# Half of the input weights by a second queue, decays turned earlier, and low parts by a product: a fused RWKV and convolutional expert kernel

## The chip, the cores and the metric

The kernel runs on one core of one Trainium2 chip. The metric is the device time of an execution in microseconds; the runs of a kernel are told by their median.

## The reference

Inputs are r, k, v, w of shape (4, 8, 768, 48) (batch, heads, steps, head size), u of (8, 48) and three weight arrays in float64: w_in (384 x 1024), conv_w (3 x 1024) and w_out (1024 x 384). For every batch and head a 48 x 48 state runs over the 768 steps:

```
y[t]  = r[t] @ (state + outer(u * k[t], v[t]))
state = w[t][:, None] * state + outer(k[t], v[t])
```

The 8 heads of a step are put side by side as a row x of 384. Then

```
h    = relu(x @ w_in)
conv = sum over j of conv_w[j] * h[t - 1 + j]      (zeros outside the sequence)
out  = (h * sigmoid(conv)) @ w_out
```

## The kernel before

The steps are cut into 24 chunks of 128 (6 for each batch). A chunk has two stages. Stage A (`stage_a`, line 531) loads w, k, r, v of the chunk with 128 partitions of 8 x 48 values (`loads`, L514, issued by SP). For each of w, k, r an ACT copy (L540) rearranges the last two heads, and three PE transposes (L546) turn the tile. DVE scans the turned decays from the end (L553), takes a reciprocal of three columns (L557, into a dA buffer), scales the keys (L558), scans from the start (L560) and scales r (L564). In the first four chunks (EARLY) the last pair of heads is gathered by twelve matmuls (L573) and an ACT copy into `last` (L576), later by six small transfers (L581). POOL forms z = r * k * u (L588, L590), DVE sums it (L591) and POOL writes it as the diagonal of pm (L594). Keys are turned back (L602, copies L604 and L605). Two ACT passes check w's bounds (L610).

Stage B (`stage_b`, line 614) carries the state. Scores go to two banks (L667; those of the last pair read `last`), DVE copies the part above the diagonal into pm (L671), the new state is made (L684, L688), and y is summed in one bank. In the first four chunks ACT copies y rounded to the reduced float32 format as the high part of x (L715), and DVE subtracts that from y to get the low part (L716). In later chunks this goes by L738 and L740.

The product stage (`block`, line 792) runs for every 384 steps, 8 blocks in all. Each of the 8 slices of 128 hidden columns takes nine matmuls (L760: three row blocks, each as high x high, high x low, low x high), the gating on ACT, DVE and POOL (L772 to L782), and the second product (L789) with an ACT copy and a store (L819, L820).

Weights arrive as float64 and are converted once, in the middle of the first chunks. w_in goes in three blocks m (`win_pieces`, line 477). Block m lands in one buffer by four transfers that SP issues: 48 rows into partitions 0 to 47 (L484), 16 rows into 48 to 63 (L488), 48 rows into 64 to 111, 16 rows into 112 to 127; a row is 8 KB. A block is then converted in three pieces of 384, 384 and 256 columns: DVE takes exponent and mantissa (L442, L450), ACT scales the exponent (L445), DVE joins them (L447, L453), POOL multiplies (L456), ACT rounds (L462), POOL takes the low part (L463). conv_w takes the same way (L470 to L475), w_out comes in three transfers of 128 partitions (L499) and eight pieces.

u is loaded ahead of everything by ACT's queue (L340); after five warm-up matmuls on zeros (L347) a product with a row of ones spreads it over the partitions (L363), and ACT copies it (L586).

The order of the instructions on each engine is written by a planner (class `Plan`, line 112). Each operation has a length from a table, tokens that it reads and writes, buffers that it holds, and a rank. The planner steps through a modelled time; a free engine takes the ready operation of the lowest rank whose buffers are to be had. Ranks are 14 for each chunk (stage B 7 later, loads 10 earlier), 10 + 5 j for piece j of w_in, 60 + 5 j for w_out, and the block's own for products. Transfers go through a model of the queues (class `Wire`, line 79). The order is then fixed: on the chip each engine runs its instructions in it and waits where data is late.

Of the kernel before, what the change touches and what calls it, by code (L numbers as in the profile page):

```python
# [9 lines left out]
F32 = mybir.dt.float32  # L10
# [12 lines left out]
WARM = 5  # L23

CHUNK, LEAD, UNIT, DOWN, PIECE = 14.0, 0.0, 5.0, 1.6, 5.0
FIRST_IN, FIRST_OUT = 10.0, 60.0
AHEAD, GUARD = 10.0, 10.0
SPREAD = (3, 5)
EARLY = 4
COLD = 60.0  # L30
CAPS = (4, 5, 3, 3, 4)
GT, TB = 1, 1
WIN = 2.0
# [8 lines left out]
    gather=1.6, carried_rows=1.4, y_rows=1.5,  # L42
    load=0.55, issue=0.45, spread=0.64,
)
TAIL = dict(PE=0.22, DVE=0.11, ACT=0.13, POOL=0.07, SP=2.2)
# [33 lines left out]
class Wire:  # L79
# [8 lines left out]
    def add(self, q, work, i, at):  # L88

        over = sum(x[0] for x in self.queues[q]) - 4.6  # L90
        self.queues[q].append([work, i, at])
        return max(0.0, over)

    def next(self):

        heads = self.heads()
        times = [q[0][2] for q in self.queues.values() if q and q[0][2] > self.t + 1e-9]
        times += [self.t + h[0] * len(heads) for h in heads]
        return min(times, default=float("inf"))
# [12 lines left out]
class Plan:  # L112
# [29 lines left out]
    def issue(self):  # L142
# [8 lines left out]
        free = dict.fromkeys(engines, 0.0)  # L151
# [5 lines left out]
        events, order, t = [], [], 0.0  # L157
# [17 lines left out]
        while len(order) < n:  # L175
            for e in engines:
# [10 lines left out]
                if e == "PE" and t < COLD:  # L187
                    us *= 1.4
# [13 lines left out]
            for i in wire.advance(t):  # L202
                heapq.heappush(events, (t + TAIL["SP"], i))
# [96 lines left out]
def rwkv_conv_moe_kernel(  # L300
# [38 lines left out]
    wide = ([fconst.tile([P, HB], F32, name=f"wide{i}") for i in range(4)], [])  # L339
    nc.scalar.dma_start(out=wide[0][0][0:1, :], in_=u.rearrange("h d -> (h d)").unsqueeze(0))  # L340


# [13 lines left out]
    make_identity(nc, ident)  # L356
    ones_f = fconst.tile([P, P], F32, name="ones_f")
# [5 lines left out]
    nc.tensor.matmul(banks[-1][:, 0:H * D], lhsT=ones_f[0:1, :], rhs=wide[0][0][0:1, :], start=True, stop=True)  # L363
# [24 lines left out]

    def kind(name, n, shape, dtype=F32, fill=None):
# [11 lines left out]
    dA_k = kind("dA", 2, [P, WID], fill=lambda t: nc.vector.memset(t, 0.0))  # L401
# [64 lines left out]
    def load_conv():  # L466
# [4 lines left out]
            out=raw.t.bitcast(I32)[0:rows, 0:2 * P], in_=conv_w.rearrange("j (t c) -> (j t) c", t=FT)), [], [(raw, 0)], [raw], moves=0.2)  # L471
# [5 lines left out]
    def win_pieces(m, piece):  # L477
# [19 lines left out]
    def wout_pieces(t0, n, piece):  # L497
# [3 lines left out]
            [], [(raw, 0)], [raw], moves=0.95 * n)  # L501
# [7 lines left out]
    def loads(n):  # L509
# [21 lines left out]
    def stage_a(n):  # L531
# [7 lines left out]
        def tr(src, t, cols):  # L539
# [4 lines left out]
            def f():  # L544
                for m in range(KT):
# [4 lines left out]
        wp, kp, rp = Buf(pa), Buf(pa), Buf(pa)  # L550
        op("DVE", "pad", lambda: nc.vector.memset(wp.t[:, 0:WID:SL], 0.0), [], [(wp, 1)], [wp])
# [3 lines left out]
            op0=ALU.mult, op1=ALU.add), [wp, (wp, 1)], [kr])  # L555
        tr(K_, kp, lambda m: kp.t[:, m * L:(m + 1) * L])
# [8 lines left out]
                                                        op=ALU.mult), [rp], [(kr, 1)], [kr])  # L565
        if n < EARLY:
# [11 lines left out]
        else:  # L578
            for g in range(2):
                for m in range(KT):  # L580
# [3 lines left out]
                        [last], moves=0.05)  # L584
# [29 lines left out]
    def stage_b(n):  # L614
# [78 lines left out]
        if early:  # L693
# [22 lines left out]
            op("DVE", "kt", lambda: nc.vector.tensor_tensor(  # L716
# [132 lines left out]
    for n in range(N + 1):  # L849
        if n < N:  # L850
# [66 lines left out]
```

## Time and profile before

| what | value |
|---|---|
| median of 3 runs | 382.01 us (379.9 to 383.73) |
| profiled execution | 381.53 us |
| its span, first to last instruction | 379.8 us |
| PE busy | 354.3 us (93%) |
| DVE busy | 281.5 us (74%) |
| ACT busy | 235.0 us (62%) |
| POOL busy | 174.9 us (46%) |
| mean granted clock of PE | 0.971 |

The span is shorter than the execution's time by 1.7 us, which lie before the first and after the last instruction. Busy shares are means over stages that differ, so the stages are to be read apart.

### The profile page before, as it was taken

How to read it: one execution, taken by the hardware profiler on the slowest of the kernel's cores; microseconds unless marked ns; L12 is line 12 of the kernel's file. 1: busy time of each engine (PE TensorE's matmuls, PEld its weight loads, DVE VectorE, ACT ScalarE, POOL GpSimd, SP SyncE). 2: the span in 40 equal slices, each digit the busy share in tenths (PEclk: the TensorE clock that was granted, in tenths of full speed). 3: DMA queues.
4: the chain of work that ended last, by engine and by line, in shares of the span. 5: the costliest groups of instructions: out<-in, count | busy, mean ns of one | idle time of the engine just before them, and what ended most of it. 6: DMA issues, size and time to landing. Idle time of an engine off the chain costs nothing.

```text
span 379.8 us, 7861 instructions
## 1 busy us (share of the span) xinstructions
PE 354.3 (93%) x2790; PEld 323.0 (85%) x2790; DVE 281.5 (74%) x575; ACT 235.0 (62%) x613; POOL 174.9 (46%) x199
## 2 busy tenths in 40 slices
PE   7977679878899999999999999999999999999994
PEld 4856568767698998999999999998999998999993
DVE  5697799998997887488787865798679845864640
ACT  6264574877768473588766753688566525765741
POOL 7293587675964343165643440454553410233430
PEclk9978888998999999999999999999999999999999
DMA  8999993322325444542542443934054121010001
GB/s 161 182 186 177 230 275 72 65 53 63 72 59 111 85 96 82 107 97 54 102 103 51 80 100 70 191 64 97 29 104 94 31 52 56 0 44 21 22 22 66
DMA packets 112802, 34.44 MB, mean 91 GB/s; under 512 B 103069, under 2 KB 110774, under 8 KB 112374
## 3 DMA queue, kind: packets, MB, share of 16 engines
q1 hardware_dynamic: 112756, 33.89, 42.0%
q8 instruction: 23, 0.38, 0.4%
q14 instruction: 21, 0.17, 0.2%
q10 hardware_dynamic: 2, 0.00, 0.0%
HBM read 25.19 MB, written 4.72 MB: 79 GB/s over the span
## 4 chain that ended last, share of the span: by engine, by line
PE 74%; DVE 9%; DMA 6%; issue 4%; ACT 3%; POOL 2%; SPq 1%; DVEq 0%; POOLq 0%
PE bank L789 26%; PE bank L760 24%; PE bank L733 5%; PE bank L667 5%; PE bank L546 4%; PE bank L723 4%; DMA r<-in_r_dram 4%; PE bank L684 2%; DMA k<-in_k_dram 2%; PE bank L602 2%; DMA wide<-in_moe_conv_w_dram 1%; DVE wide L447 1%; DVE g L779 1%; DVE a L774 1%; POOL wide L456 1%
## 5 line engine op out<-in xcount | busy, mean ns | idle before, releaser
L789 PE MATMUL bank<-wo,gh 128*128 128x384 f32 x576 | 125.7, 345 | 2.0 <-POOL wo L463 1.0
L760 PE MATMUL bank<-xT,wi 128*128 128x386 f32 x576 | 125.2, 346 | 0.2 <-DVE xT L716 0.2
L782 POOL TENSOR_TENSOR gh<-g,gh 128x384 fp32r<-128x384 f32 x64 | 64.5, 1012 | 107.2 <-ACT gh L781 104.2
L789 PEld LDWEIGHTS bank<-wo,gh 128*128 128x128 f32 x576 | 100.1, 189 | 4.9 <-issue 1.3
L760 PEld LDWEIGHTS bank<-xT,wi 128*128 128x128 f32 x576 | 100.2, 188 | 3.2 <-issue 1.8
L774 DVE SCALAR_TENSOR_TENSOR a<-bank,cw,a 128x384 f32<-128x384 f32 x64 | 38.3, 608 | 20.4 <-ACT a L773 20.4
L778 ACT ACTIVATE a<-a 128x384 f32<-128x384 f32 x64 | 33.3, 522 | 27.0 <-DVE a L776 27.0
L594 POOL TENSOR_SCALAR_AFFINE_SELECT pm<-dg 128x1024 f32<-128x1024 f32 x24 | 26.3, 1095 | 48.2 <-PE bank L733 38.7
L779 DVE TENSOR_TENSOR g<-bank,a 128x384 f32<-128x384 f32 x64 | 34.5, 547 | 13.8 <-ACT a L778 13.1
L772 ACT ACTIVATE bank<-bank 128x386 f32<-128x386 f32 x64 | 30.5, 477 | 22.1 <-PE bank L760 21.2
L781 ACT CAST gh<-g 128x384 fp32r<-128x384 f32 x64 | 32.4, 511 | 12.9 <-DVE g L779 12.6
L671 DVE COPY_PREDICATED pm<-upper,bank 128x512 f32<-128x512 int32 x48 | 33.4, 725 | 8.5 <-PE bank L667 8.4
L776 DVE SCALAR_TENSOR_TENSOR a<-bank,cw,a 128x384 f32<-128x384 f32 x64 | 38.5, 610 | 0.6
L773 ACT ACTIVATE a<-bank,cw 128x384 f32<-128x384 f32 x64 | 36.5, 580 | 0.6
L553 DVE TENSOR_TENSOR_SCAN kr<-bank,one_end 128x387 f32<-128x387 f32 x24 | 22.9, 956 | 15.0 <-PE bank L546 15.0
L588 POOL TENSOR_TENSOR z<-r,k 128x384 f32<-128x384 f32 x24 | 24.3, 1014 | 19.6 <-DMA r<-in_r_dram 19.6
L590 POOL TENSOR_TENSOR z<-z,ubc 128x384 f32<-128x384 f32 x24 | 24.2, 1007 | 1.3
L667 PEld LDWEIGHTS bank<-kr 48*128 48x128 f32 x288 | 18.7, 189 | 6.9 <-issue 4.5
L667 PE MATMUL bank<-kr 48*128 48x128 f32 x288 | 23.7, 291 | 0.5 <-DVE wide L453 0.4
L560 DVE TENSOR_TENSOR_SCAN kr<-bank,dA 128x387 f32<-128x387 f32 x24 | 22.8, 952 | 0.1
L733 PE MATMUL bank<-pm,v 128*48 128x128 f32 x320 | 22.3, 282 | 0.0
L819 ACT COPY wide<-bank 128x384 f32<-128x384 f32 x24 | 11.5, 479 | 16.4 <-PE bank L789 16.0
(108 smaller groups left out, 529.0 us busy)
## 6 DMA issues: line engine op xcount, KB each, us to landing
w<-in_w_dram SPq DMA_DIRECT2D x24, 192.0 KB, 2.9
k<-in_k_dram SPq DMA_DIRECT2D x24, 192.0 KB, 3.6
r<-in_r_dram SPq DMA_DIRECT2D x24, 192.0 KB, 3.8
v<-in_v_dram SPq DMA_DIRECT2D x24, 192.0 KB, 3.0
out_dram<-wide SPq DMA_DIRECT2D x24, 192.0 KB, 2.0
gh<-in_moe_w_in_dram SPq DMA_DIRECT2D x6, 384.0 KB, 6.5
gh<-in_moe_w_out_dram SPq DMA_DIRECT2D x2, 1152.0 KB, 7.4
last<-kr SPq DMA_DIRECT2D x120, 16.2 KB, 1.8
```

The costliest lines, as they stand in the source:

```text
L667: nc.tensor.matmul(sc[g].t[:, m * L:(m + 1) * L], lhsT=kt(m)[p], rhs=rt(m)[p], start=True, stop=True)
L671: op("DVE", "cp", lambda g=g: nc.vector.copy_predicated(out=pm.t[:, g], mask=upper.unsqueeze(1).to_broadcast([P, NP, L]), data=sc[g].t.rea ...
L733: nc.tensor.matmul(y.t[rows, cs], lhsT=vf[:, h * D:h * D + rows.stop - rows.start], rhs=pm.t[:, g, m, :], start=(c == 0 and m == 0), stop= ...
L760: nc.tensor.matmul(t.t[:, 0:HB + 2], lhsT=wi[:, m, a, f * P:(f + 1) * P], rhs=xT[:, x0 + m, c, xs], start=(m == 0 and j == 0), stop=(m == ...
L773: ("ACT", "mul", lambda: nc.scalar.mul(out=a(), in_=h(1), mul=cw[:, 1, bass.ds(f, 1)]), [t, "cw"], [a1]),
L774: ("DVE", "stt", lambda: nc.vector.scalar_tensor_tensor(out=a(), in0=h(0), scalar=cw[:, 0, bass.ds(f, 1)], in1=a(), op0=ALU.mult, op1=ALU. ...
L776: ("DVE", "stt", lambda: nc.vector.scalar_tensor_tensor(out=a(), in0=h(2), scalar=cw[:, 2, bass.ds(f, 1)], in1=a(), op0=ALU.mult, op1=ALU. ...
L778: ("ACT", "sig", lambda: nc.scalar.activation(out=a(), in_=a(), func=AF.Sigmoid), [], [a1]),
L779: ("DVE", "gate", lambda: nc.vector.tensor_tensor(out=g.t[:, 0:width], in0=h(1), in1=a(), op=ALU.mult), [t, a1], [g]),
L781: ("ACT", "cast", lambda: nc.scalar.copy(out=part(0)[:, 0:width], in_=g.t[:, 0:width]), [g], [key]),
L782: ("POOL", "lo", lambda: nc.gpsimd.tensor_tensor(out=part(1)[:, 0:width], in0=g.t[:, 0:width], in1=part(0)[:, 0:width].bitcast(F32), op=AL ...
L789: nc.tensor.matmul(acc.t[:, 0:DM], lhsT=part(a)[:, tt * P:(tt + 1) * P], rhs=wo[:, f, c, :], start=(f == 0 and a + c == 0), stop=(f == FT ...
```

## The change

The lower 48 rows of each w_in block stay on SP's queue, the upper 48 (partitions 64 to 111) are issued by ACT, block 0's after the copy of chunk 0's k, block m's after that of chunk m + 1's w. w_in's blocks and the filter weights are entered into the plan one chunk later, with ranks 14 + 6 j for w_in and 65 + 6 j for w_out. In chunks 1 to 3 padding, turning and first scan of the decays have a rank lower by 10. u is loaded by ACT as an operation of the plan, and its product stands behind chunk 0's turned r. There are nine warm-up matmuls, and one dA buffer. The low part of x in the first four chunks is made by a product of the high part with a negated identity, added into y's bank, and an ACT copy. The planner's model has other numbers: transfers have a share of the engines and places in a ring, and engines begin later. The diff, cut to its core:

```diff
-WARM = 5
+WARM = 9
-CHUNK, LEAD, UNIT, DOWN, PIECE = 14.0, 0.0, 5.0, 1.6, 5.0
-FIRST_IN, FIRST_OUT = 10.0, 60.0
+CHUNK, LEAD, UNIT, DOWN, PIECE = 14.0, 0.0, 5.0, 1.6, 6.0
+FIRST_IN, FIRST_OUT = 14.0, 65.0
-COLD = 60.0
+COLD = ((9.9, 1.8), (60.0, 1.3))
-WIN = 2.0
+RING = 192
+FIRST = 10.0
-TAIL = dict(PE=0.22, DVE=0.11, ACT=0.13, POOL=0.07, SP=2.2)
+TAIL = dict(PE=0.22, DVE=0.11, ACT=0.13, POOL=0.07, SP=1.4)
+BEGIN = dict(PE=4.3, DVE=2.4, ACT=3.0, POOL=5.0, SP=0.8)
...
-    def add(self, q, work, i, at):
-        over = sum(x[0] for x in self.queues[q]) - 4.6
-        self.queues[q].append([work, i, at])
-        return max(0.0, over)
+    def add(self, q, moves, i, at):
+        work, share, places = moves
+        over, held = sum(x[4] for x in self.queues[q]) + places - RING, 0.0
+        for x in self.queues[q]:
+            if over <= 0:
+                break
+            over -= x[4]
+            held += x[0]
+        self.queues[q].append([work, i, at + 0.7, share, places])
+        return held
+    def pace(self, heads):
+        return 1.0 / max(1.0, sum(h[3] for h in heads))
...
-                if e == "PE" and t < COLD:
-                    us *= 1.4
+                if e == "PE":
+                    us *= next((x for until, x in COLD if t < until), 1.0)
...
-                heapq.heappush(events, (t + TAIL["SP"], i))
+                heapq.heappush(events, (t + (0.8 if self.ops[i][5][2] == 64 else TAIL["SP"]), i))
...
-    nc.scalar.dma_start(out=wide[0][0][0:1, :], in_=u.rearrange("h d -> (h d)").unsqueeze(0))
...
+    less = fconst.tile([P, P], F32R, name="less")
+    nc.scalar.mul(out=less, in_=ident, mul=-1.0)
...
-    nc.tensor.matmul(banks[-1][:, 0:H * D], lhsT=ones_f[0:1, :], rhs=wide[0][0][0:1, :], start=True, stop=True)
...
-    dA_k = kind("dA", 2, [P, WID], fill=lambda t: nc.vector.memset(t, 0.0))
+    dA_k = kind("dA", 1, [P, WID], fill=lambda t: nc.vector.memset(t, 0.0))
...
-        for g in range(2):
-            op("SP", "issue", lambda g=g: nc.sync.dma_start(
+        for g, (eng, queue) in enumerate((("SP", nc.sync), ("ACT", nc.scalar))):
+            r0 = (6 + g) * D + 16 * m
+            op(eng, "issue", lambda g=g, queue=queue: queue.dma_start(
                 out=row()[64 * g:64 * g + D, 0:2 * DF], in_=w_in[(2 * m + g) * D:(2 * m + g + 1) * D, :]),
-                [], [(raw, 2 * g)], [raw], moves=WIN * 0.75)
-            r0 = (6 + g) * D + 16 * m
+                [(chunks[m + 1]["w"] if m else chunks[0]["k"], 1)] if g else [], [(raw, 2 * g)], [raw], moves=(2.3, 0.5, 4))
             op("SP", "issue", lambda g=g, r0=r0: nc.sync.dma_start(
                 out=row()[64 * g + D:64 * g + 64, 0:2 * DF], in_=w_in[r0:r0 + 16, :]),
-                [], [(raw, 2 * g + 1)], [raw], moves=WIN * 0.25)
+                [], [(raw, 2 * g + 1)], [raw], moves=(1.2, 0.5, 2))
...
         wp, kp, rp = Buf(pa), Buf(pa), Buf(pa)
+        rank = plan.rank
+        plan.rank = rank - (FIRST if 0 < n < EARLY else 0.0)
         op("DVE", "pad", lambda: nc.vector.memset(wp.t[:, 0:WID:SL], 0.0), [], [(wp, 1)], [wp])
         tr(W, wp, lambda m: wp.t[:, m * SL + 1:m * SL + 1 + L])
         op("DVE", "scan", lambda: nc.vector.tensor_tensor_scan(
...
             op0=ALU.mult, op1=ALU.add), [wp, (wp, 1)], [kr])
+        plan.rank = rank
         tr(K_, kp, lambda m: kp.t[:, m * L:(m + 1) * L])
...
+        if n == 0:
+            ut, row = Buf(pb), chunks["u"]
+            op("PE", "ones", lambda: nc.tensor.matmul(ut.t[:, 0:H * D], lhsT=ones_f[0:1, :], rhs=row.t[0:1, :],
+                                                      start=True, stop=True), [(R_, 1), row], [ut])
+            op("ACT", "kh", lambda: nc.scalar.copy(out=ubc.rearrange("p h d -> p (h d)"), in_=ut.t[:, 0:H * D]), [ut], ["ubc"])
...
-        if n == 0:
-            op("ACT", "kh", lambda: nc.scalar.copy(out=ubc.rearrange("p h d -> p (h d)"), in_=banks[-1][:, 0:H * D]),
-               [(K_, 1)], ["ubc"])
...
             op("ACT", "kh", lambda: nc.scalar.copy(out=xT[:, 0:KT, 0, ts], in_=thirds(y.t)), [y], [("x", odd, c, 0)])
-            op("DVE", "kt", lambda: nc.vector.tensor_tensor(
-                out=xT[:, 0:KT, 1, ts], in0=thirds(y.t), in1=xT[:, 0:KT, 0, ts].bitcast(F32), op=ALU.subtract),
-                [y, ("x", odd, c, 0)], [("x", odd, c, 1)])
+            op("PE", "rest", lambda: nc.tensor.matmul(thirds(y.t), lhsT=less, rhs=xT[:, 0:KT, 0, ts], start=False, stop=True,
+                                                      skip_group_check=True), [("x", odd, c, 0)], [y])
+            op("ACT", "kh", lambda: nc.scalar.copy(out=xT[:, 0:KT, 1, ts], in_=thirds(y.t)), [y], [("x", odd, c, 1)])
...
+    plan.rank = -2 * AHEAD
+    chunks["u"] = Buf(val_k)
+    op("ACT", "issue", lambda: nc.scalar.dma_start(out=chunks["u"].t[0:1, :], in_=u.rearrange("h d -> (h d)").unsqueeze(0)),
+       [], [chunks["u"]], moves=(0.05, 1.0, 4))
...
-            if n < KT:
-                plan.rank = FIRST_IN + PIECE * KT * n
-                win_pieces(n, piece)
-                if n == 0:
+            if 0 < n <= KT:
+                plan.rank = FIRST_IN + PIECE * KT * (n - 1)
+                win_pieces(n - 1, piece)
+                if n == 1:
                     load_conv()
-            if n == KT - 1:
+            if n == KT:
                 for t0 in range(0, FT, 3):
```

## Rows read from the trace of the kernel before

**Rows 1.** The page's part 2: 40 slices of 9.5 us, DVE and DMA.

```profile
DVE  5697799998997887488787865798679845864640
...
DMA  8999993322325444542542443934054121010001
```

**Rows 2.** Stretches: busy time of each engine, granted clock, DMA share, GB/s.

```profile
core 0: us, PE busy (x) PEld busy (x) DVE busy (x) ACT busy (x) POOL busy (x), PEclk, DMA share, GB/s
0.00:12.80 12.80, 10.28 (x38) 6.94 (x40) 5.36 (x18) 6.93 (x21) 9.76 (x33) 1.00 0.90 172
12.80:45.00 32.20, 25.80 (x253) 21.60 (x251) 26.34 (x58) 15.41 (x52) 16.22 (x18) 0.84 1.02 195
45.00:60.00 15.00, 10.88 (x94) 9.44 (x95) 14.58 (x34) 10.19 (x34) 11.87 (x13) 0.79 0.83 215
60.00:102.00 42.00, 35.24 (x258) 29.86 (x257) 40.81 (x85) 31.05 (x77) 30.82 (x32) 0.95 0.32 65
102.00:374.00 272.00, 271.93 (x2155) 255.21 (x2153) 194.39 (x384) 170.81 (x432) 106.21 (x105) 1.00 0.33 71
```

**Rows 3.** Waits of DVE until 105 us: total us, times, longest us.

```profile
DVE kr L553 <- PE bank L546: 6.3, 2, 3.4
DVE wide L447 <- ACT bank L445: 2.8, 4, 2.0
```

**Rows 4.** Timeline (start us, us) of chunks 0 and 1, 7.7 to 15 us.

```profile
7.72 0.27 ACT L540 COPY w<-w 128x96 f32<-128x96 f32 x1 [0.63 <-DMA w<-in_w_dram]
...
8.26 2.91 PE L573 MATMUL bank<-kr,sel 128*112 128x130 f32 x12 [1.24 <-DVE bank L551]
...
9.16 1.09 POOL L594 TENSOR_SCALAR_AFFINE_SELECT pm<-dg 128x1024 f32<-128x1024 f32 x1 [1.30 <-DVE dg L591]
...
11.60 0.85 PE L546 MATMUL bank<-ident,w 128*128 128x128 f32 x3
...
12.48 0.96 DVE L553 TENSOR_TENSOR_SCAN kr<-bank,one_end 128x387 f32<-128x387 f32 x1 [3.40 <-PE bank L546]
...
14.57 1.31 DVE L671 COPY_PREDICATED pm<-upper,bank 128x512 f32<-128x512 int32 x2
```

**Rows 5.** Timeline of the filter weights' transfer and first conversion.

```profile
28.83 0.39 SPq L470 DMA_DIRECT2D wide<-in_moe_conv_w_dram  x1
...
35.40 0.28 DVE L442 TENSOR_SCALAR bank<-wide 24x128 int32<-24x128 int32 x1 [1.99 <-DMA wide<-in_moe_conv_w_dram]
```

**Rows 6.** Timeline of ACT and DVE, 39 to 43 us.

```profile
39.83 0.27 ACT L540 COPY w<-w 128x96 f32<-128x96 f32 x1 [2.92 <-DMA w<-in_w_dram]
...
42.02 0.55 DVE L447 SCALAR_TENSOR_TENSOR wide<-gh,bank 128x384 int32<-128x384 int32 x1 [1.98 <-ACT bank L445]
```

**Rows 7.** Stretches in which one kind of transfer prevails: loads, w_in, w_out.

```profile
3.00:8.00 5.00, 3.93 (x11) 2.01 (x11) 2.44 (x4) 2.85 (x11) 4.34 (x14) 1.00 1.05 204
11.00:16.00 5.00, 4.64 (x49) 3.66 (x49) 3.45 (x6) 1.12 (x4) 1.21 (x2) 1.00 1.00 157
...
48.00:50.00 2.00, 2.00 (x12) 1.98 (x10) 2.00 (x5) 1.96 (x8) 1.59 (x3) 0.50 0.99 374
```

**Rows 8.** Groups until 102 us, shapes apart: busy us, mean ns of one.

```profile
L760 PE MATMUL bank<-xT,wi 128*128 128x386 f32 x81 | 17.0, 350 | 0.2 <-DVE xT L716 0.2
...
L716 DVE TENSOR_TENSOR xT<-bank,xT 128x384 fp32r<-128x384 f32 x4 | 2.2, 548 | 0.0
...
L715 ACT CAST xT<-bank 128x384 fp32r<-128x384 f32 x4 | 2.0, 489 | 0.0
...
L347 PE MATMUL bank<-junk 128*128 128x384 bf16 x5 | 1.8, 522 | 1.2 <-DVE table L351 1.2
L363 PE MATMUL bank<-wide,ones_f 1*128 1x384 f32 x2 | 1.6, 923 | 0.0
```

**Rows 9.** Timeline: the one issue on ACT's queue.

```profile
0.82 0.51 ACTq L340 DMA_DIRECT2D wide<-in_u_dram  x1
```

**Rows 10.** Timeline: the first products of block 0.

```profile
61.31 1.69 PE L760 MATMUL bank<-xT,wi 128*128 128x386 f32 x8 [0.18 <-DVE xT L716]
```

More of the change, by code (lines that the diff above doesn't have):

```diff
@@ L41 @@
     z=0.98, diag=1.07, lo=0.97,
-    gather=1.6, carried_rows=1.4, y_rows=1.5,
+    gather=1.6, rest=0.3, carried_rows=1.4, y_rows=1.5, ones=0.8,
     load=0.55, issue=0.45, spread=0.64,
 )
-TAIL = dict(PE=0.22, DVE=0.11, ACT=0.13, POOL=0.07, SP=2.2)
+TAIL = dict(PE=0.22, DVE=0.11, ACT=0.13, POOL=0.07, SP=1.4)
+BEGIN = dict(PE=4.3, DVE=2.4, ACT=3.0, POOL=5.0, SP=0.8)
 class Buf:
@@ L97, in next @@
         times = [q[0][2] for q in self.queues.values() if q and q[0][2] > self.t + 1e-9]
-        times += [self.t + h[0] * len(heads) for h in heads]
+        times += [self.t + h[0] / self.pace(heads) for h in heads]
         return min(times, default=float("inf"))
@@ L150, in issue @@
         ready = {e: [] for e in engines}
-        free = dict.fromkeys(engines, 0.0)
+        free = dict(BEGIN)
         locked = dict(DVE=0.0, POOL=0.0)
@@ L156, in issue @@
                 ready[self.ops[i][0]].append((self.ops[i][7], i))
-        events, order, t = [], [], 0.0
+        events, order, t = [(x, -1) for x in BEGIN.values()], [], 0.0
+        heapq.heapify(events)
         def places(bufs):
@@ L386, in rwkv_conv_moe_kernel @@
     nc.vector.memset(ebias, -916.0 * 2.0 ** 23)
+    wide = ([fconst.tile([P, HB], F32, name=f"wide{i}") for i in range(4)], [])
     def kind(name, n, shape, dtype=F32, fill=None):
@@ L470, in load_conv @@
         op("SP", "issue", lambda: nc.sync.dma_start(
-            out=raw.t.bitcast(I32)[0:rows, 0:2 * P], in_=conv_w.rearrange("j (t c) -> (j t) c", t=FT)), [], [(raw, 0)], [raw], moves=0.2)
+            out=raw.t.bitcast(I32)[0:rows, 0:2 * P], in_=conv_w.rearrange("j (t c) -> (j t) c", t=FT)), [], [(raw, 0)], [raw], moves=(0.2, 1.0, 2))
         from_double(lambda: raw.t.bitcast(I32)[0:rows, 0:2 * P], lambda: val.t[0:rows, 0:P], P, [raw, (raw, 0)], [val], rows)
@@ L500, in wout_pieces @@
             out=raw.t[:, 0:n, :], in_=w_out[t0 * P:(t0 + n) * P, :].rearrange("(t p) c -> p t c", p=P)),
-            [], [(raw, 0)], [raw], moves=0.95 * n)
+            [], [(raw, 0)], [raw], moves=(0.95 * n, 1.0, 8 * n))
         for t in range(n):
@@ L514, in loads @@
             op("SP", "load", lambda nm=nm, src=src: nc.sync.dma_start(
-                out=st[nm].t[:, :, 0:D], in_=src[b, :, s, :].rearrange("h t d -> t h d")), [], [st[nm]], moves=1.15)
+                out=st[nm].t[:, :, 0:D], in_=src[b, :, s, :].rearrange("h t d -> t h d")), [], [st[nm]], moves=(0.97, 1.0, 64))
     def seg(t, at):
@@ L583, in stage_a @@
                         in_=kr.t[64 * g + D:64 * g + 64, :, m * SL:m * SL + SL + 1]), [kr, (kr, 1)], [(last, g, m)],
-                        [last], moves=0.05)
-        if n == 0:
-            op("ACT", "kh", lambda: nc.scalar.copy(out=ubc.rearrange("p h d -> p (h d)"), in_=banks[-1][:, 0:H * D]),
-               [(K_, 1)], ["ubc"])
+                        [last], moves=(0.05, 1.0, 4))
         op("POOL", "z", lambda: nc.gpsimd.tensor_tensor(out=z.t, in0=R_.t[:, :, 0:D], in1=K_.t[:, :, 0:D], op=ALU.mult),
@@ L752, in stage_b @@
                     [t for x in cs for t in (("spare", x), ("x", odd, x, 1))], [("x", odd, x, 2 + 3 * g + m) for x in cs],
-                    moves=0.1 * len(cs))
+                    moves=(0.1 * len(cs), 1.0, 4))
     def product_in(t, f, m, x0, xs, wi=wi):
@@ L819, in block @@
             op("ACT", "out", lambda acc=acc, o=o: nc.scalar.copy(out=o.t, in_=acc.t[:, 0:DM]), [acc], [o])
-            op("SP", "issue", lambda o=o, rows=rows: nc.sync.dma_start(out=out[b, rows, :], in_=o.t), [o], [], moves=1.0)
+            op("SP", "issue", lambda o=o, rows=rows: nc.sync.dma_start(out=out[b, rows, :], in_=o.t), [o], [], moves=(1.0, 1.0, 8))
     def moe_block(x0, s0, width, moe, ps, dst):
```

4 lines of the change are left out of this document (2 added, 2 removed).

## The prediction

> **What bounds the kernel now.** I read the page's slices first, then the stretches, then who waited for whom, then the timeline where the longest waits lie. The slices show three stages [rows 1]: the DMA engines are full for the first six slices, some 57 us, and are then half idle; DVE is at 8 to 9 tenths from the second to the eleventh slice. The stretches give this in numbers [rows 2]. From 102 us to 374 PE is busy 271.93 of 272 us: nothing but PE's own work counts there, and the end is the moment at which that state begins plus the work left. From 60 to 102 PE lacks 6.8 us (42 less 35.24) while DVE is busy 40.81 of 42, and from 45 to 60 DVE is busy 14.58 of 15. So from 45 to 102 DVE decides when PE becomes full, and a microsecond of DVE time saved ahead of 102, in work or in idle time, is a microsecond of the end, as long as ACT (31.05 of 42) and POOL (30.82 of 42) don't take over. DVE's idle time ahead of that is what can be won: 3.4 us in one wait before 12.8 [rows 4], 32.2 less 26.34 = 5.9 us from 12.8 to 45 and 0.4 from 45 to 60, 9.7 in all. What it waits for is PE's turned decays, ACT, and a transfer [rows 3, 5]. [...]
>
> The sums are made against the profiled execution, 381.5 us (a span of 379.8 and 1.7 around it); the median of the runs shown is 382.0, 0.5 above.
>
> **1. Early turned decays.** W(1), the decays of chunk 1, are in place at 7.72 (ACT then copies for 0.27), but PE first does the gather of chunk 0 from 8.26 on (2.91 us) and turns W(1) only at 11.60. DVE's first scan of chunk 1 starts at 12.48 after 3.40 us of nothing [rows 4]. With its rank lowered by 10 the turning goes ahead of the gather: 8.0 plus the 0.85 that it takes at this place, so the scan can start at about 9.1. DVE then has two scans of some 0.96 us and a reciprocal to put in the gap, about 2.1 us. Against it stands that the gather ends up to 0.85 later, and with it the scores that read `last`. What is late next is the first weight block, and DVE gets it earlier only by part 2. Bounds: -0.85 (nothing fills the gap, the gather is late) and +3.4 (the whole wait); I take 1.5, nearer to what the two scans hold. For chunks 2 and 3 the same edit moves work inside stretches in which DVE has other work, and I count nothing.
>
> **2. Upper halves of w_in on a second queue.** One block m moves 2 x 384 KB and 2 x 128 KB, 1.05 MB. While it runs (11 to 16 us) the DMA engines are busy all the time and move 157 GB/s; loads of r, k, v, w run at 204 GB/s, and w_out at 374, at the same busy share [rows 7]. So w_in is not slow for lack of requests: its engines wait while they are busy. At 157 GB/s a block costs 6.7 us, three cost 20. The two 384 KB parts (0.79 MB) cost 5.0 of the 6.7. If the halves, now side by side on two queues, go at up to the rate of w_out, they take 2.1; if the limit is the engines themselves, still 5.0. So between 0 and 2.9 us for each block. I take 2.5 (double the rate of 157) for blocks 1 and 2, whose upper halves follow the copy of chunk 2's and chunk 3's w and so come when SP has about reached the lower ones, and half of that for block 0, whose upper half runs beside chunk 1's loads: 6.2 us of DMA time, ends 0 and 8.7. [...]
>
> That time is not the end's by itself; it is worth what DVE waits for. Two waits can be told. DVE stood 1.99 us, until 35.40, for the filter weights, issued at 28.83 between the transfers of block 2 [rows 5]: with shorter transfers ahead of it, and with the planner's larger cost for them, the conversion is asked for nearer to its landing. Bounds 0 and 2.0; I take 1.5. And at 40.0 DVE stood 1.98 us for ACT's exponents, which stood behind ACT's copy of w, itself waiting 2.92 us for its load [rows 6]; all such waits for L445 are 2.8 us [rows 3]. Loads behind w_in land earlier by what w_in saves, up to 6.2 us, so this wait should go. Bounds 0 and 2.8; I take 1.5, since an order made anew leaves a wait somewhere else. The rest of the 5.9 us I leave where it is.
>
> **3. Low parts by a product.** Four DVE subtractions of 548 ns go, 2.2 us [rows 8]. Three lie where DVE is short of time soon after, one (at 19.9) ahead of waits that would swallow it: 1.6 taken, ends 0 and 2.2. In their place come four matmuls of 384 columns; the nearest, L760, is busy 17.0 us in 81, so 0.21 each and 0.84 in all, at most four times the 350 ns that one takes by itself, 1.4. PE has 4.1 us idle from 45 to 60 and 6.4 from 12.8 to 45 [rows 2], so this is covered; uncovered it would cost those 0.84. And four ACT copies like L715 [rows 8], 489 ns each, 2.0 us. ACT is busy 15.41 of 32.2 and 10.19 of 15 us there [rows 2], but exponents that DVE waits for stand behind it. With three issues on ACT's queue at the 0.51 us of the one shown [rows 9] and the copy for the negated identity, ACT gets some 3.9 us more. Bounds 0 and -3.9; I take -0.3, the nearest row being half-idle ACT. For chunk 3 the low part is waited for at once: PE stood 0.18 us for DVE's last part [rows 10]. The new path is matmul (0.35) and copy (0.49) instead of one 0.55, so 0.3 later: -0.3, ends 0 and -0.5.
>
> **4. u, warm-up, buffers.** u's product leaves the place ahead of W(0), where it took 1.6 us, and four warm-up matmuls come in at 1.8/5 = 0.36 each, 1.4 us [rows 8]: W(0) is turned at about the same time. The product then stands between R(0) and the gather, where W(1) and a wait stood anyway. z needs u later by up to 2 us; the diagonal it ends in was written from 9.16 on and DVE's use of it began at 14.57 [rows 4], which covers this. Cost 0, ends -1.6 and +0.2. One dA buffer instead of two only matters if a reciprocal would go ahead of the previous chunk's second scan; in the rows of part 1 it follows its own scan at once: 0, ends 0 and -1.0 (one scan). The matmuls of the gather ran at 2.91 us for 12 although the granted clock says 1.00 in that stretch [rows 2, 4]; more warm-up might end that earlier, and I count nothing.
>
> **Sum.** 1.5 + 1.5 + 1.5 + 1.6 - 0.3 - 0.3 = 5.5 us, so 381.5 - 5.5 = 376.0 for a profiled execution, and 376.5 about the median; I say 376. The upper ends together give 10.6 us, the lower ones -8.7; all idle time of 9.7 with the 2.2 of the subtractions would be 11.9.
>
> **Rivals.** First, the second queue brings nothing. Against it: w_out moves 374 GB/s at the same busy share. For it: the engines show no idle time while w_in runs. Then loads behind w_in land as before, the waits for the filter weights and for ACT stay, and part 1 and 3 alone leave 1.5 + 1.6 - 0.6 = 2.5 us: 379.0, or 380 to 381 where the new order puts a wait in the place of the 3.4. [...] No run here has two w_in halves in flight from two queues, so the trace doesn't decide.
>
> Second, slower: upper halves jump the queue. On one queue w_in waits its turn behind the loads; on ACT's queue it starts at once, and chunk 1's loads, which part 1 needs early, share the engines with it. If it doesn't run faster, each upper half holds back the loads by its 384 KB at 157 GB/s, 2.5 us, three times 7.5, and the early turning is lost. With the 1.6 of part 3 kept this is 381.5 + 5.9 = 387; with one of three covered 385. It decides where W(1) lands: later than about 10.2 instead of 7.7, and the scan of chunk 1 is no earlier than now. For it: loads are 1.05 of full busy share from 3 to 8 us, there is no room. Against it: block 0's upper half is behind K(0) on ACT, so chunk 0 is safe, and DVE has no other use for the gap.
>
> Third, all of DVE's idle time goes because the new costs of transfers give an order without such waits: near 381.5 - 10 = 371.5. For it: the waits are those of an order that asked for data before it was there. Against it: each wait removed has moved work up to the next transfer.
>
> **How the numbers follow.** Forecast 0.45 (its own range 373 to 379.5), second queue without effect 0.24, slower 0.16, all idle time gone 0.15. The range reaches from 371 (a third of the last case below it) to 383.5 (most of the slower case above it): about 0.18 is left out. Runs of the kernel before lie 1% apart, so about 1% is what can be told from no change: 378.2 and 385.8. Below lie 0.40 of the forecast, all of the last case and 0.05 of the first rival: 0.60. Above lie 0.12 of the slower case. Between, 0.28.
>
> **What would show it.** Right: W(1) is turned by about 9.5 and DVE's wait of 3.4 is under 1.5; w_in's stretches show 250 GB/s or more; no wait of DVE for the filter weights over 1 us; L760 starts by 56 instead of 61; PE is full from about 96 instead of 102. Wrong: w_in still at 157 GB/s (first rival), W(1) landing after 10 (second), or DVE's idle time up to 60 us still above 8 us with other names on it. The forecast falls too if PE is not full after 102, since then the end isn't set by the early part.

## The result and the profile after

The changed kernel takes 376.49 us (median of 4 runs, 376.34 to 377.23) against 381.56 us (4 runs, 379.9 to 383.73) beside it: a ratio of 0.9866, 95% interval 0.9825 to 0.9907. The profiled execution took 376.34 us with a span of 374.6, 5.2 less than the span before. The forecast was 376.0.

Lines have moved: turning of a tile is now L559, first scan L568, z's sum L609, gather L594, conversion L454, L457, L459, L465, w_in's parts L498 and L501, high part, product and low part of x L733, L734, L736, first product L778. First the totals and slices of the page, to be held against the table before and [rows 1].

```profile
PE 350.3 (93%) x2798; PEld 319.8 (85%) x2798; DVE 282.9 (76%) x570; ACT 236.4 (63%) x618; POOL 174.9 (47%) x199
...
PE   7777888878999999999999999999999999999994
...
DVE  4795989999998793997779684888877845664630
...
DMA  8999992343234343633344441634344031010001
```

PE's slices before, which [rows 1] leaves out:

```profile
PE   7977679878899999999999999999999999999994
```

PE's busy time fell by 4.0 us (354.3 to 350.3), its idle time by 1.2 (25.5 to 24.3): together the 5.2. DVE has 2.2 us of subtractions less and yet is busy longer (282.9 for 281.5), so its total says nothing. DMA is full until the same slice. The stretches, columns as in [rows 2]:

```profile
0.00:12.80 12.80, 9.48 (x58) 5.96 (x60) 6.09 (x19) 7.12 (x22) 7.93 (x32) 1.00 0.95 179
12.80:45.00 32.20, 25.76 (x271) 21.72 (x271) 26.76 (x63) 19.08 (x63) 19.87 (x22) 0.95 1.09 192
45.00:60.00 15.00, 13.25 (x100) 11.67 (x98) 13.88 (x29) 10.30 (x33) 11.27 (x13) 0.77 0.86 242
60.00:102.00 42.00, 34.91 (x271) 29.88 (x269) 41.72 (x87) 31.99 (x81) 29.40 (x31) 0.96 0.33 66
102.00:360.00 258.00, 257.74 (x2061) 241.75 (x2061) 193.91 (x375) 165.99 (x418) 105.38 (x104) 1.00 0.34 73
```

The stretch from 60 to 102 us hides where PE becomes full. It is full from 90 us on: busy 5.97 of 6 us from 90 to 96 and 6.00 from 96 to 102, where the kernel before had 4.82 and 4.66. So the last state begins 12 us earlier, one slice in the rows of PE above. But up to 90 us PE had stood idle 18.6 us, for 17.3 before, so that its idle time in all fell by only 1.2. How much was done by 102, where both kernels are full, can be compared directly: 374.6 less 102 leaves 272.6 us of PE's work, where 277.8 were left before. Ahead of 102, PE was busy 1.2 us longer (83.40 for 82.19), and its mean granted clock from 12.8 to 45 us was 0.95 for 0.84, so that more of that time was at the level of 1.00 and less at that of 0.50 (which both kernels show from 37 to 38 us). The clock is the larger share. PE's busy time multiplied by its mean granted clock is nearly the same in both kernels (354.3 x 0.971 = 344.0, 350.3 x 0.981 = 343.6), so by this estimate the 4.0 us of busy time are time that the lower level cost before and no longer costs. The count of first products up to 102 says the same in work, beside 81 in [rows 8]:

```profile
L778 PE MATMUL bank<-xT,wi 128*128 128x386 f32 x99 | 22.0, 365 | 0.5 <-DVE wide L465 0.5
```

18 more products at the 0.21 us of [rows 8] are 3.8 of the 5.2 us. They come from block 0's start; its first 24 were done before the scores of chunk 4, while before the first stood at 60.7 us:

```profile
54.08 0.44 PE L734 MATMUL bank<-xT,less 128*128 128x384 f32 x1 [1.25 <-ACT xT L733]
...
54.93 4.51 PE L778 MATMUL bank<-xT,wi 128*128 128x386 f32 x24
59.37 0.94 PE L685 MATMUL bank<-kr 48*128 48x128 f32 x12
```

Chunk 3's scores stand at 43.4 us now and stood at 50.3 before; the planner put them ahead of all of the last block of w_in (DVE starts its first piece at 45.85), where they stood behind that block's first piece before (joined at 48.80). DVE's waits until 105 us, beside [rows 3]:

```profile
DVE kr L568 <- POOL sel L380: 2.9, 1, 2.9
DVE dg L609 <- POOL z L608: 2.6, 1, 2.6
DVE bank L454 <- DMA wide<-in_moe_conv_w_dram: 2.1, 1, 2.1
DVE wide L459 <- ACT bank L457: 1.8, 2, 1.1
DVE sd L664 <- ACT last L597: 1.6, 1, 1.6
```

The scan's wait of 3.4 us is gone (the 2.9 on top is the start of chunk 0, 2.95 before), but a wait of 2.6 us for z has come in nearly the same place. The filter weights are waited for 2.1 us, as before (1.99). ACT's exponents cost 1.8 for 2.8, and a wait for `last` of 1.6 us is new. The start of chunk 1 on PE, ACT and DVE, beside [rows 4]:

```profile
7.31 0.92 PE L594 MATMUL bank<-kr,sel 128*112 128x130 f32 x6
...
8.43 0.92 PE L594 MATMUL bank<-kr,sel 128*112 128x130 f32 x6 [0.19 <-DVE kr L580]
...
9.51 0.49 PE L559 MATMUL bank<-ident,w 128*128 128x128 f32 x3
```
```profile
7.81 0.27 ACT L553 COPY w<-w 128x96 f32<-128x96 f32 x1 [1.20 <-DMA w<-in_w_dram]
...
9.33 0.46 ACT L586 COPY ubc<-bank 128x384 f32<-128x384 f32 x1
```
```profile
10.96 0.55 DVE L609 TENSOR_REDUCE dg<-z 128x8 f32<-128x384 f32 x1 [2.59 <-POOL z L608]
11.43 0.95 DVE L568 TENSOR_TENSOR_SCAN kr<-bank,one_end 128x387 f32<-128x387 f32 x1
```

W(1) is still turned behind the gather, not ahead of it; it comes at 9.51 because the gather takes twice 0.92 us instead of 2.91. The scan could follow at 10.0, but DVE's order has z's sum ahead of it, and z waits for u, whose product now stands behind R(0) (0.91 us from 6.47) and is copied by ACT only at 9.33, behind W(1)'s copy and two passes that check bounds: the scan starts at 11.43, 1.05 us earlier than before. The transfers, first the issues of w_in's two halves on ACT's and SP's queues, then a stretch as in [rows 7]:

```profile
5.05 0.33 ACTq L498 DMA_DIRECT2D gh<-in_moe_w_in_dram  x1
...
22.20 0.32 ACTq L498 DMA_DIRECT2D gh<-in_moe_w_in_dram  x1
...
25.98 0.32 ACTq L498 DMA_DIRECT2D gh<-in_moe_w_in_dram  x1
```
```profile
7.86 2.75 SPq L498 DMA_DIRECT2D gh<-in_moe_w_in_dram  x1
...
17.42 1.57 SPq L498 DMA_DIRECT2D gh<-in_moe_w_in_dram  x1
...
34.38 1.11 SPq L498 DMA_DIRECT2D gh<-in_moe_w_in_dram  x1
```
```profile
11.00:16.00 5.00, 3.45 (x48) 2.80 (x49) 4.93 (x10) 1.30 (x5) 3.05 (x3) 1.00 1.09 174
```

The halves of a block are issued 2.8, 4.8 and 8.4 us apart. From issue to landing they take 5.8 to 7.5 us, so the first two pairs are side by side for a part of the time and the third not at all. The rate is 174 GB/s, not 250. The times from issue to landing (least, median, most):

```profile
DMA to landing us min/median/max: 5.8/6.3/7.5
```

### The profile page after: what moved, and what is told of

It reads as the page before. It is cut to its first block, busy times and chain, and to the rows that moved or that the text cites. A ratio compares the mean times of both kernels' runs of the same rounds, so it can differ in the third digit from the quotient of the medians.

```text
span 374.6 us, 7881 instructions
## 1 busy us (share of the span) xinstructions
PE 350.3 (93%) x2798; PEld 319.8 (85%) x2798; DVE 282.9 (76%) x570; ACT 236.4 (63%) x618; POOL 174.9 (47%) x199
## 4 chain that ended last, share of the span: by engine, by line
PE 72%; DMA 11%; DVE 8%; SPq 3%; ACT 2%; issue 1%; POOL 1%; DVEq 0%; POOLq 0%
PE bank L807 26%; PE bank L778 24%; DMA r<-in_r_dram 9%; PE bank L685 5%; PE bank L751 5%; PE bank L559 4%; PE bank L741 4%; PE bank L702 2%; SPq L602 2%; PE bank L620 2%; DMA w<-in_w_dram 1%; DMA last<-kr 1%; SPq L527 1%; DVE pm L689 1%; DVE g L797 1%
## 5 line engine op out<-in xcount | busy, mean ns | idle before, releaser
L778 PE MATMUL bank<-xT,wi 128*128 128x386 f32 x576 | 126.5, 348 | 0.5 <-DVE wide L465 0.5
L778 PEld LDWEIGHTS bank<-xT,wi 128*128 128x128 f32 x576 | 101.8, 191 | 2.9 <-issue 1.3
L568 DVE TENSOR_TENSOR_SCAN kr<-bank,one_end 128x387 f32<-128x387 f32 x24 | 22.9, 956 | 5.1 <-POOL sel L380 2.9
L608 POOL TENSOR_TENSOR z<-z,ubc 128x384 f32<-128x384 f32 x24 | 24.3, 1014 | 4.3 <-ACT ubc L586 3.4
L468 POOL TENSOR_TENSOR wide<-wide,wide 128x384 f32<-128x384 f32 (+2 forms) x18 | 16.8, 936 | 12.2 <-DVE wide L465 11.7
## 6 DMA issues: line engine op xcount, KB each, us to landing
last<-kr SPq DMA_DIRECT2D x120, 16.2 KB, 1.8
```

Of the source, the lines that this page charges most:

```text
L778: nc.tensor.matmul(t.t[:, 0:HB + 2], lhsT=wi[:, m, a, f * P:(f + 1) * P], rhs=xT[:, x0 + m, c, xs], start=(m == 0 and j == 0), stop=(m == ...
```

## The experiments

Two readings are left by this. Either each part of the change brings what it removes, with other sizes than forecast; or most of the gain is the new order as a whole, which the parts, the new ranks and the planner's new costs make together. Undoing a part so that the order of all instructions stays prices the part alone; undoing it so that the planner writes another order prices both. All ratios are to the kernel before, run beside. The difference of two ratios has the uncertainty of both (the root of the sum of the squares of their half intervals): 2.7 to 3.0 us for the three kernels that undo a part with the order kept, 2 to 2.5 us for the others that start from the changed kernel, 1.0 to 1.1 for the kernel before against itself.

**w_in's transfers alone.** The kernel holds only these transfers: two blocks, loaded in five ways one after the other, and none of the reference's computation.

```diff
+    def parts(m, lo, up, small):
+        for g, q in enumerate((lo, up)):
+            q.dma_start(out=t[64 * g:64 * g + D, :], in_=w_in[(2 * m + g) * D:(2 * m + g + 1) * D, :])
+            (small or q).dma_start(out=t[64 * g + D:64 * g + 64, :], in_=w_in[r0:r0 + 16, :])
...
+    parts(m, nc.sync, nc.sync, None)
+    parts(m, nc.sync, nc.scalar, nc.sync)
+    parts(m, nc.sync, nc.scalar, None)
...
+    nc.sync.dma_start(out=raws[m], in_=w_in[128 * m:128 * m + 128, :])
```

The first three ways are the calls of `parts`: one queue, the upper 48 rows by ACT, the whole upper half by ACT. In the fourth both queues load into partitions 0 to 63, of two buffers; the fifth is one transfer over all 128 partitions.

> Two blocks of w_in (2.1 MB) are loaded five times, one after the other, with nothing else on the chip: (1) all on SP's queue as before, (2) the upper 48 rows on ACT's queue as in the change, (3) each half wholly on its own queue, (4) two queues, both into partitions 0 to 63, (5) one transfer of 128 partitions per block on one queue. Nothing else of the kernel is computed. If the halves of the partitions are the limit: about 160 to 190 GB/s in (1) and (4), 250 to 370 in (3), something between in (2), 350 or more in (5). If transfers to disjoint halves serialize whichever engine issues them: (2), (3) and (4) like (1).

The middle of each phase, in the same order (one run):

```profile
5.00:17.00 12.00, 4.22 (x4) 0.00 (x0) 1.00 1.03 155
21.00:31.00 10.00, 0.15 (x1) 0.00 (x0) 1.00 1.04 197
35.00:45.00 10.00, 0.15 (x1) 0.00 (x0) 1.00 1.00 182
50.00:62.00 12.00, 0.15 (x1) 0.00 (x0) 1.00 1.02 163
67.00:71.00 4.00, 0.15 (x1) 0.00 (x0) 1.00 0.97 406
```

The DMA engines are busy throughout in every phase. One queue gives 155 GB/s, the rate of [rows 7]; halves side by side give 182 to 197, 1.2 to 1.3 times; two queues into one half give 163, nothing; a transfer over all partitions 406, 2.6 times; that one is also longer, 1 MB for each block. From the first issue to DVE's first use of the last data the phases took 16.2, 14.0, 14.1, 15.9 and 7.4 us, so two queues save about 1 us for each block, where the forecast had 2.5. So the halves neither double nor leave the rate alone: the doubling was the author's estimate, and of the two cases expected the one in which halves serialize comes nearer, with 182 to 197 for 155, a fifth to a quarter to win.

**The second queue undone, same order.**

```diff
-for g, (eng, queue) in enumerate((("SP", nc.sync), ("ACT", nc.scalar))):
+for g, (eng, queue) in enumerate((("SP", nc.sync), ("ACT", nc.sync))):
```

> The changed kernel with its order kept, but the upper halves issued by SP at the places of the plan. Theory A (the order of DVE's work makes the gain): within 1 us of the changed kernel's 376.5. Theory B (the second queue makes it): 379 or more, the last w_in block lands 2 us or more later, and block 0's first product starts later than 55.5 us.

377.63 us (4 runs), ratio 0.9881 (0.9823 to 0.9938). The difference from 0.9866 is 0.6 us, within both intervals. The stretch that showed 174 GB/s shows 175:

```profile
11.00:16.00 5.00, 3.86 (x51) 3.02 (x51) 4.93 (x10) 0.53 (x3) 3.05 (x3) 1.00 1.14 175
```

So most of the gain stays without the second queue; what the queue itself is worth is 0.6 us, uncertain by 2.7. One sign that was named for the queue did come: block 0's first product starts at 56.24 us, later than 55.5. DVE's wait for ACT's exponents is 4.5 us, for 1.8, and that for the filter weights 1.3, for 2.1. The last transfers of w_in are issued only 0.2 us later.

**The low parts back on DVE, same order.**

```diff
-            op("PE", "rest", lambda: nc.tensor.matmul(thirds(y.t), lhsT=less, ...
+            op("PE", "rest", lambda: None, [("x", odd, c, 0)], [y])
-            op("ACT", "kh", lambda: nc.scalar.copy(out=xT[:, 0:KT, 1, ts], in_=thirds(y.t)), ...
+            op("ACT", "kh", lambda: nc.vector.tensor_tensor(out=xT[:, 0:KT, 1, ts],
+                in0=thirds(y.t), in1=xT[:, 0:KT, 0, ts].bitcast(F32), op=ALU.subtract), ...
```

> The changed kernel with its order kept, but the low parts subtracted by DVE again at the places where the plan has ACT's second copy; no product. The prediction's part 3: 1.0 to 1.6 us worse, 377.5 to 378. If DVE's place in the queue doesn't matter there: 376.5 or, as ACT gets 2 us back, a little less.

376.1 us (4 runs), ratio 0.9861 (0.9798 to 0.9924): the product shows no gain, -0.2 us, uncertain by 2.9. Block 0 starts at 54.7 us with the subtraction and at 54.9 with the product. The changed kernel's longest wait of PE until 105 us:

```profile
PE bank L734 <- ACT xT L733: 2.9, 3, 1.2
```

PE stands three times for ACT's rounding ahead of the product; with the subtraction it stood 2.6 us for the same rounding, once, ahead of block 0.

**Five warm-up matmuls instead of nine, same order.**

```diff
-WARM = 9
+WARM = 5
```

> The changed kernel with five warm-up matmuls instead of nine, the order kept. Theory C (PE's full speed from the first transposes on makes part of the gain): transposes of K(0) and R(0) take 0.85 to 0.9 again instead of 0.55, and 377.5 to 378.5. Theory A: 376 to 377, since chunk 0 is not what chunk 3 waits for.

377.71 us (4 runs), ratio 0.9871 (0.9803 to 0.9939): 0.2 us by the ratios, 1.2 by the medians. The gather took its old time again, W(1) was turned at 11.91, and z's wait grew to 5.4 us:

```profile
8.54 2.94 PE L594 MATMUL bank<-kr,sel 128*112 128x130 f32 x12
11.27 0.85 PE L620 MATMUL bank<-ident,kr 128*128 128x128 f32 x3
11.91 0.85 PE L559 MATMUL bank<-ident,w 128*128 128x128 f32 x3
```

Chunk 1 came 2.4 us later and the end by 0.2, uncertain by 3.0. That fits a microsecond at the start not being one at the end, but it doesn't show it; the next kernel does.

**Nine warm-up matmuls in the kernel before, same order.** The counterpart.

```diff
-WARM = 5
+WARM = 9
```

> The kernel before with nine warm-up matmuls instead of five, and the same order. With the change's order, five instead of nine cost about 1.2 us. If the warm-up is worth something by itself (K(0) and R(0) turned and the gather run at full speed, 0.9 us instead of 2.9): 379.5 to 381, the wait of 3.4 us for the turned decays of chunk 1 under 2 us. If W(0) now merely waits behind more warm-ups: 382 to 383.5.

381.71 us (10 runs), ratio 0.9998 (0.9972 to 1.0024). W(0) waits behind the warm-ups, everything up to chunk 1's scan is 1.29 us later (13.77 for 12.48), and the end is the same within 1.0 us. The wait for the filter weights shrank from 2.0 to 0.9 us and that for ACT's exponents from 2.8 to 1.5:

```profile
DVE wide L447 <- ACT bank L445: 1.5, 3, 1.1
...
DVE bank L442 <- DMA wide<-in_moe_conv_w_dram: 0.9, 1, 0.9
```

These two waits gave up 2.4 us, more than the delay: what is early at the start is waited away there.

**The old ranks of the weight pieces in the new kernel; another order.**

```diff
-CHUNK, LEAD, UNIT, DOWN, PIECE = 14.0, 0.0, 5.0, 1.6, 6.0
-FIRST_IN, FIRST_OUT = 14.0, 65.0
+CHUNK, LEAD, UNIT, DOWN, PIECE = 14.0, 0.0, 5.0, 1.6, 5.0
+FIRST_IN, FIRST_OUT = 10.0, 60.0
```

> The changed kernel with the old ranks of the weight pieces (10 + 5 j and 60 + 5 j), planned anew. Theory A: most of the gain goes, 379.5 to 381.5, chunk 3's scores move back behind w_in's last pieces and block 0's first product starts at 58 us or later. Theory B: 376 to 377.5.

380.2 us (10 runs), ratio 0.9956 (0.9914 to 0.9998): 3.4 us of the 5, uncertain by 2.2, are gone. Chunk 3's scores are back at 53.1 us and block 0 begins at 60.7.

**The new ranks in the kernel before; another order.** The edit is the reverse.

```diff
-CHUNK, LEAD, UNIT, DOWN, PIECE = 14.0, 0.0, 5.0, 1.6, 5.0
-FIRST_IN, FIRST_OUT = 10.0, 60.0
+CHUNK, LEAD, UNIT, DOWN, PIECE = 14.0, 0.0, 5.0, 1.6, 6.0
+FIRST_IN, FIRST_OUT = 14.0, 65.0
```

> The kernel before with nothing but the new ranks of the weight pieces (14 + 6 j and 65 + 6 j), planned anew with the old model. Theory A: chunk 3's scores move ahead of w_in's last pieces, block 0's first product starts at 58 us or sooner instead of 60.7, and the time is 378 to 380. If the ranks only work with the new model of transfers: 381 to 383.

381.91 us (10 runs), ratio 1.0004 (0.9975 to 1.0033). Block 0 begins at 56.2, nearly as early as after, and nothing is won, since PE is busy 34.16 us from 60 to 102 for 35.24 before. An early first product by itself is not the gain.

**No early rank for the turned decays; another order.**

```diff
-FIRST = 10.0
+FIRST = 0.0
```

> The changed kernel without the lower rank of the early decays (FIRST = 0), planned anew. The prediction's part 1: 1.5 us worse, 378. Theory A (the ranks of the weight pieces make the gain): 376 to 377, since the changed kernel turned W(1) only at 9.51 and scanned it at 11.43, so little was won at that place.

379.55 us (8 runs), ratio 0.9947 (0.991 to 0.9983): 3.1 us of the gain, uncertain by 2.1, are gone, twice the term of the forecast. But W(1) is turned at 9.51 in this kernel too, behind the gather, so the wait that the term was worked out from is not where it was lost. DVE was busy 39.88 us from 60 to 102 for 41.72 in the changed kernel.

**Filter weights entered one chunk later; another order.** An attempt at a better version, at the wait of 2.1 us.

```diff
-                if n == 1:
+                if n == 2:
                     load_conv()
```

> The changed kernel with the filter weights entered one chunk later still, behind block 1's pieces, planned anew. DVE's wait of 2.1 us for them at 32.6 should go, and with it up to 2 us of the end: 374.5 to 376. If DVE only waits for block 1's data in its place: 376 to 377.

380.47 us (10 runs), ratio 0.9977 (0.9947 to 1.0007). The wait fell to 1.7 us, and those for ACT's exponents rose from 1.8 to 4.0.

Three re-plannings had each lost 3 us or more, whatever was undone. If that is the order's doing, a re-planning that undoes nothing should lose as much. The last three kernels tell the two readings apart.

**Pieces spaced by 6.3 instead of 6.0.** No part is undone.

```diff
-CHUNK, LEAD, UNIT, DOWN, PIECE = 14.0, 0.0, 5.0, 1.6, 6.0
+CHUNK, LEAD, UNIT, DOWN, PIECE = 14.0, 0.0, 5.0, 1.6, 6.3
```

> Every part of the change stays; only the spacing of the weight pieces' ranks goes from 6.0 to 6.3, which means nothing to the work but makes the planner write another order. Theory A (most of the gain is this one order, not the parts): the time leaves 376.5 and lands where the re-planned kernels did, 378.5 to 381. Theory B (the parts and the later ranks carry the gain, and undoing any of them costs what that part is worth): within 1 us of 376.5.

389.79 us (4 runs), ratio 1.022 (1.0169 to 1.0272): 13 us slower than the changed kernel, with every part of the change in place, and outside what either reading gave. Its order has the filter weights' issue behind a load that was itself held; SP's queue, then DVE's first conversion:

```profile
31.42 5.04 SPq L527 DMA_DIRECT2D w<-in_w_dram  x1
36.55 6.24 SPq L482 DMA_DIRECT2D wide<-in_moe_conv_w_dram  x1
42.89 0.38 SPq L527 DMA_DIRECT2D v<-in_v_dram  x1
```
```profile
44.44 0.28 DVE L454 TENSOR_SCALAR bank<-wide 24x128 int32<-24x128 int32 x1 [5.28 <-DMA wide<-in_moe_conv_w_dram]
```

The issue was held for 6.24 us, and DVE stood 5.28 us for data that came at 34.67 in the changed kernel. Up to 102 us DVE was busy 77.99 us, for 88.47.

**PE's early instructions taken as 1.35 times their length instead of 1.3.** Only the planner's cost changes.

```diff
-COLD = ((9.9, 1.8), (60.0, 1.3))
+COLD = ((9.9, 1.8), (60.0, 1.35))
```

> Every part and every rank stays; the planner only takes PE's early instructions as 1.35 times their length instead of 1.3 before 60 us, so the order differs from some 20 us on. Theory A (the order itself): 378 to 381, and the first product of block 0 later than 54.9 us or DVE less busy than 88.5 us up to 102. Theory B (the parts): within 1 us of 376.5.

375.56 us (4 runs), ratio 0.9839 (0.9812 to 0.9866): the fastest of all, faster than before for certain, from the changed kernel (0.9825 to 0.9907) not told apart. So each reading missed once: the changed order is no single lucky point, as the second theory says, and the parts don't secure the gain, as the first says.

**The old costs in the planner.** All moves of the change stay.

```diff
-    def add(self, q, moves, i, at):
+    def add(self, q, work, i, at):
...
-COLD = ((9.9, 1.8), (60.0, 1.3))
+COLD = ((60.0, 1.4),)
...
-moves=(0.97, 1.0, 64)
+moves=1.15
```

> All moves of the change stay (second queue, early decays, product, u, ranks), but the planner's costs are those of the kernel before: old transfer prices, no ring, engines that begin at 0, one factor of 1.4 before 60 us. Theory A (the order itself): 379 to 382, as much lost as by undoing a part. Theory B (the parts): 376 to 378, since the parts are all there.

384.23 us (10 runs), ratio 1.005 (1.002 to 1.008): 7 us slower than the changed kernel by the ratios and slower than the kernel before, although all the moves are in it. DVE's longest wait is again that for the filter weights:

```profile
DVE bank L443 <- DMA wide<-in_moe_conv_w_dram: 6.6, 1, 6.6
```

**All kernels side by side.** DVE's busy time up to 102 us is from the stretch 0 to 102 of each trace; where the subtractions stand on DVE, their 2.2 us [rows 8] are taken off, so that the column counts the same work.

| kernel | order | DVE busy to 102, same work | span |
|---|---|---|---|
| PE's factor 1.35 | new | 89.1 | 372.8 |
| changed kernel | | 88.5 | 374.6 |
| one queue | kept | 87.3 | 376.0 |
| low parts on DVE | kept | 87.1 | 374.4 |
| filter weights later | new | 86.0 | 377.7 |
| no early rank | new | 85.4 | 376.8 |
| five warm-ups | kept | 85.1 | 377.6 |
| before, nine warm-ups | kept | 85.1 | 380.3 |
| old ranks | new | 85.1 | 380.1 |
| before | | 84.9 | 379.8 |
| before, new ranks | new | 84.4 | 379.6 |
| old costs | new | 79.6 | 384.5 |
| pieces by 6.3 | new | 78.0 | 388.4 |

The span follows the column over its whole length, 1.3 us for each microsecond (a straight line through the 13 points, which lie within 1.7 us of it). It is a count of progress, not a proof of cause, but it says in which place to look: work that DVE gets done by 102 us.

PE's granted clock is a rival measure, and no run holds it fixed. It is 0.981 to 0.985 in the three shortest of these executions and 0.960 to 0.972 in the six longest, but also 0.985 with five warm-ups and 0.966 without the early rank, which lie between. With one order alone it moves the time by less than the difference between the orders: over 55 executions of the kernel before, run beside the experiments, it lies between 0.955 and 0.983, and the span falls by about 1.1 us for each 0.01 (correlation -0.45). Whether an order that keeps PE busier gets the higher clock, or the higher clock lets DVE get further by 102 us, these runs don't tell apart.

## Why the prediction was right, and where its steps were not

The total was right, 5.5 us forecast and 5.2 measured between the profiled spans; the sum by which it was reached was not, so that the agreement is luck. No term can be shown to have brought its amount, and what brought most of the gain had no term.

- **What bounds the kernel.** PE is full after 102 us as said, in the changed kernel already from 90, and DVE's work up to 102 ranks the kernels nearly. The step that failed is that "a microsecond of DVE time saved ahead of 102, in work or in idle time, is a microsecond of the end". The first 12 us don't count like that: 1.29 us later there cost nothing, within 1.0, in the kernel before, where the waits between 33 and 42 us, for the filter weights and for ACT behind a load, gave up 2.4. In the changed one 2.4 us later cost 0.2 by the ratios and 1.2 by the medians; there the first of these waits shrank to 1.2 and the second grew to 2.7, so where the delay went is open. It should have been asked of each saved microsecond which wait stands behind it before 102. PE's granted clock had no term; by the estimate above the lower level accounts for 4.0 of the 5.2 us, and whether it is a limit or a consequence of PE's idle time stays open.
- **Part 1.** The price of 1.5 was for the turning of W(1) moving ahead of the gather, and it did not move; the scan gained 1.05 us through the faster gather, which was seen and counted as nothing. Without the early rank 3.1 us are lost, in another order; as neutral re-plannings moved the time by -1 and +13 us, that says nothing of the part alone. Its own price stays open.
- **Part 2.** Failed. The rate of 2 x 157 supposed that the halves would be side by side. They are issued 2.8 to 8.4 us apart, and no run shows the double rate from which the 2.5 us for each block were taken: even side by side they reach 182 to 197 GB/s, 1.2 to 1.3 times one queue's 155, and save about 1 us for each block. The wait for the filter weights stayed (2.1 for 1.99), the wait for ACT's exponents lost 1.0 of the 1.5 taken, and another of 1.6 came. The queue as a whole is worth 0.6 us, uncertain by 2.7, where the terms said 3.0. With one queue the wait for the filter weights is even shorter (1.3) and that for the exponents longer (4.5), so the second term may be the queue's in part.
- **Part 3.** Not seen. Its three terms together, 1.6 - 0.3 - 0.3 = 1.0, were measured at -0.2, uncertain by 2.9, so that 1.0 is not excluded either. The four products took PE 1.8 us (445 ns each), more than the 1.4 named as the most. What the path through ACT costs is not shown: PE waits for ACT's rounding 2.9 us with the product and 2.6 without.
- **Part 4.** u was priced at 0 with the write of the diagonal as cover, ends -1.6 and +0.2. The cover was not there: DVE's order has z's sum ahead of chunk 1's scan and waits 2.6 us for it, most of it for ACT, since the product is done at 7.38 and copied at 9.33. What that costs in the end no run shows; it lies in the first 12 us.
- **The order.** The forecast set "an order made anew leaves a wait somewhere else" against the waits removed, and gave the new ranks and costs no term. Undoing the queue, the product and four warm-ups with the order kept moved the time by 0.6, -0.2 and 0.2 us, and each of these kernels is still faster than before, with its interval below 1; no run undoes all three together. Each re-planning of the changed kernel that undid something lost 3 us or more, the old costs 7; of two that undid nothing, one lost 13 and the other came out 1.0 lower. So the runs show that what decides is which order the planner writes, and that its new costs and ranks had to be there for this one. Which of the order's many moves carries the gain is not shown; the two orders that lost most have the wait for the filter weights at 5.3 and 6.6 us, but the others have it at 2.8 or less and differ all the same.

Of the rivals, the first had its mechanism right (no gain shown from the queue, 174 GB/s for 157) and its time wrong (379 to 381), since the gain came from elsewhere. The second fell: W(1) landed at 7.81 us, 0.09 later than before. The third fell as well: DVE's idle time counted as in the forecast is 9.1 us (2.6 and 5.4 and 1.1) for 9.7. That is over the 8 us named as a sign against the forecast, which came true while the total held: DVE did 3.6 us more of the same work by 102, 2.2 of it in place of the subtractions.

Of the signs, W(1) by 9.5, block 0 by 56 and PE full from 96 were seen (9.51, 54.93 and 90), the first for another reason than the one given and with a wait of 2.6 us for z in place of the one of 3.4; 250 GB/s and no wait for the filter weights were not.

## What to carry to other kernels

Where a planner writes the order, a change of moves and a change of order are two things: test each part with the order kept, and re-plan with a cost or rank changed by a few per cent, before a part is given the credit. Here neutral changes of the planner's numbers gave 375.6 and 389.8 us, a spread larger than any part; so several orders are worth timing, and what to look at in each is the work that the limiting engine gets done by a fixed time near the start of the final state, and PE's granted clock with it. A mean over a long stretch can hide where that state begins: here only slices of 6 us showed it. An idle microsecond is priced by the next wait behind it, not by its length.

## What the runs showed of the hardware that was not expected

The granted clock is 1.00 from 0 to 12.8 us in the profiles of the kernels before and after, yet the matmuls of that stretch have two lengths. After the nine warm-ups three transposes take 0.85 us at 4.05 and 0.55 at 5.22; with five they take 0.90 at 5.35 and 0.85 still at 11.91, and 0.55 from 15.29 on. What decides when they become short is open: with the same nine warm-ups ahead, k's transposes at 5.22 took 0.90 with one queue, and in the kernel before with nine warm-ups transposes took 0.85 until 12.88.

SP's queue held issues for times that differ: the issue of the filter weights took 0.39 us in the kernel before, 0.67 in the changed one, 3.33 with one queue, and 6.24 with pieces by 6.3, where the DMA engines show 8 and 9 tenths in every slice of 0.78 us until 42.1, and SP's next issue came at 42.89.
